# A float64 weight split without a sign pass, weight columns by halves, a third staging place, p in packs, and a new table of ranks

## The chip, the cores and the metric

The kernel runs on one core of one Trainium2 chip. The metric is the device time in microseconds (us), the median of several runs. Matrix products run on PE (TensorE), elementwise work on DVE (VectorE) and ACT (ScalarE), and loads and stores are issued by SP. POOL does almost nothing here. "clock" is the clock that TensorE was granted; its two levels are 2.4 GHz (shown as 1.00) and 1.2 GHz (0.50).

## The reference

`p` holds 32 packed queries for each of 8 x 8 heads. They attend to `k` and `v`, the result serves as keys and values for `q`, and a gated feed-forward layer with a convolution over the sequence follows. The scale factors of the weights are float64 scalars of NumPy, so `w_in`, `conv_w` and `w_out` arrive as float64; `q`, `k`, `v` and `p` are float32.

```python
def sm_attn(qq, kk, vv):
    s = scale * np.matmul(qq, kk.transpose(0, 1, 3, 2))
    s = s - np.max(s, axis=-1, keepdims=True)
    a = np.exp(s)
    a = a / (np.sum(a, axis=-1, keepdims=True) + 1e-09)
    return np.matmul(a, vv)
p_packed = sm_attn(p, k, v)          # q, k, v: 8, 8, 576, 64; p: 8, 8, 32, 64
out = sm_attn(q, p_packed, p_packed)
x = out.transpose(0, 2, 1, 3).reshape(8, 576, 512)
h = np.maximum(x @ w_in, 0.0)        # w_in: 512 x 1024
conv_out = conv_w[0] * h_before + conv_w[1] * h + conv_w[2] * h_after
gate = 1.0 / (1.0 + np.exp(-conv_out))
return (h * gate @ w_out).astype(np.float32)   # w_out: 1024 x 512
```

## The kernel before

**Groups and batches.** The 64 heads are worked on in 16 groups g of four heads; two groups make one of the 8 batches b. For a group, `load_kq` and `load_v` load `k`, `q` and `v`, and `head_transpose` turns `k` and `q` (the first four groups on PE with copies by ACT, the others on DVE). `queries` scales and transposes the packed queries. `attention` does the rest: first scores (tiles `kT`, `pT`), their maximum (`nm` on DVE), the exponential, the product with `v`, second scores (`qT`, `ppT`), and a softmax on DVE and ACT whose last tiles are `a2hi` and `a2lo`, a value and its remainder.

**The feed-forward part.** `packed_weight(b, hf)` multiplies the packed values of a batch with one half of the columns of `w_in` and leaves `ghi` and `glo`. `ffn1(b, j)`, j from 0 to 7, multiplies these with `a2hi` and `a2lo`, applies the ReLU into one of three buffers `hbuf`, and gates it with the convolution's sigmoid into `hgt`. `ffn2(m)`, m from 0 to 35, splits 128 rows of `hgt` into `xhi` (ACT) and `xlo` (DVE) and multiplies them with `wo_hi` and `wo_lo` in 24 matmuls (L720). Its output goes out by DMA.

**The weights.** `load_weight(i)` and `weight(i)` handle eight pieces of 1 MB: four of `w_in`, then four of `w_out`. `f64_parts` splits a float64 piece into float32 parts: ACT scales the high words (L281), and DVE shifts left by 3 (L283), puts the sign bit back (L285), masks the exponent (L289) and scales the low words (L291). PE adds the parts up (L346). The pieces are staged in halves of `hgt[1]` (`spare`), one of them in `w_in_sb`. `packed_weight` waits for all four pieces of `w_in`.

**What sets the order.** `Flow` is a planner in the kernel. Each function yields its work as steps for an engine; whenever an engine is free, the ready step with the lowest number in the table `RANKS` goes next, and the order is then fixed: each engine runs its list in turn, SP its list of loads and stores too. `take` and `give` are buffers handed on: three tiles `kq` for `k` and `q`, two for `v`, three `hbuf` (`h`), and so on. Until the first `ffn2` has been placed, the planner fills gaps of PE with small matmuls on the tile `idle` (L258), which compute nothing that is used.

Of the kernel before, what the change touches and what calls it, by code (L numbers as in the profile page):

```python
# [8 lines left out]
F32 = mybir.dt.float32  # L9
# [12 lines left out]
    k=[-645.37, -581.7, -645.95, -844.11, -379.62, -375.1, -363.45, -47.77, 708.11, 1034.07, -210.35, 1035.0, 2258.89, 1246.95, 2776.42, 5491.81],  # L22
    v=[-634.88, -576.04, -524.23, -352.44, -474.91, 569.37, 815.34, 1122.01, 1500.35, 1611.47, 1083.29, 1634.37, 1803.36, 2006.67, 5057.89, 5016.42],
    q=[-504.47, 5384.4, -435.54, -367.64, -409.72, -123.0, -229.45, 1157.76, 1826.35, 1958.61, 1961.31, 2349.96, 2739.02, 5189.37, 5900.17, 5687.45],
    queries=[-124.07, 4947.56, -576.16, 695.08, -936.2, 3146.3, -805.71, -833.64, 1723.01, 937.55, -839.58, -1636.16, -699.27, 4760.45, 746.56, -516.14],
    kT=[1289.34, 1260.73, 824.17, 1514.37, 3387.98, 1162.59, 1714.67, -880.73, 2085.08, 5733.43, 661.28, -243.54, -133.19, -1560.99, 2719.23, 1444.35],
    qT=[2349.41, -862.23, 1500.3, -520.73, -836.19, 1311.15, 5046.28, 2258.92, 84.63, 1578.67, 2671.05, 1256.34, 4798.98, -604.41, 2193.41, 4803.19],
    attention=[-312.33, 1080.14, -1264.6, -854.22, -833.2, 888.88, 1206.99, 641.08, -62.4, -943.58, 2495.68, -762.92, -896.54, 638.89, -844.03, -837.43],
    sums=[1170.39, 4739.32, 1087.43, -129.08, -833.34, -795.65, -617.55, 732.0, 92.96, 1253.68, 921.66, 4676.98, 2791.9, -198.77, 1508.38, -128.03],
# [1 line left out]
    load=[-1419.97, -236.8, -646.87, 5205.55, 2444.58, -393.65, -586.49, -453.41],
    weight=[958.54, 4407.77, 746.18, 4155.56, 1719.93, 2554.0, -847.43, 4425.27],
    packed=[-838.33, 1929.06, 1148.03, -461.0, 4425.27, 4993.29, 668.7, 1234.53, -222.7, 5473.37, -518.74, 1316.77, 884.48, 5592.56, 5384.7, 1490.18],
    ffn1=[1814.15, -1369.6, -784.93, 4729.05, 5596.18, 845.36, 1618.07, 1158.66, -659.35, 1633.27, 4246.81, -514.28, 1503.84, -125.71, 542.72, -819.28, -857.94, -834.32, 831.55, -551.42, -551.12, -846.96, 1932.67, -543.96, 4461.75, 3236.12, 773.89, -616.98, -320.81, 5019.89, -713.12, -601.27, -1230.08, -655.85, 1159.65, 2700.73, 2122.97, 4279.32, -792.92, 18.96, 1213.31, -1515.25, 5098.64, -153.63, -504.19, -419.06, 1111.01, 1722.91, -533.48, 1251.79, 710.95, -783.68, -384.13, 5910.7, -565.69, 4602.14, 659.94, 497.38, 1568.93, -811.33, 2444.88, 589.46, 5595.83, 4931.48],
# [751 lines left out]
```

## Time and profile before

| | us |
|---|---|
| median of three runs | 434.65 |
| lowest and highest | 433.1 and 435.48 |
| the profiled execution, its own time | 435.47 |
| its span, first to last instruction | 433.6 |

In the profile a busy time is the union of an engine's instructions. Instructions of one engine overlap a little at their edges, so a row's duration is longer than the step from one start to the next. A matmul's end is modelled, so a full PE is not PE at its peak. A wait in brackets names the time that the engine sat idle before an instruction and who ended it. Line numbers are those of the kernel before unless they are said to be of the kernel after.

### The profile page before, as it was taken

The page shows a single profiled execution, that of the slowest core. Times are in us where ns is not written, and L with a number is a line of the kernel's source. Part 1 is how long each engine was busy: PE and PEld are TensorE (multiplying, and loading weights), DVE is VectorE, ACT ScalarE, POOL GpSimd, SP SyncE. Part 2 cuts the span into 40 slices and gives each one's busy share as a digit, 9 for nine tenths or more (in the row PEclk, how much of TensorE's full clock was granted, in tenths as well). Part 3 has the DMA queues.
Part 4 walks back from the last instruction along what each step waited for, and adds up shares of the span by engine and source line. Part 5 has one row for each costly group of instructions (what it writes and reads, how often), then busy time and mean ns, then how long its engine had stood idle before and what let it go on. Part 6 is the DMA issues. An engine that isn't in the chain of part 4 may idle for free.

```text
span 433.6 us, 8375 instructions
## 1 busy us (share of the span) xinstructions
PE 420.9 (97%) x3437; PEld 336.9 (78%) x3437; DVE 351.5 (81%) x497; ACT 321.4 (74%) x509; POOL 1.6 (0%) x13
## 2 busy tenths in 40 slices
PE   5999999799999999999999999999999999999996
PEld 5676878578876987787877888788869787897774
DVE  3479998879999999999999987998688994685220
ACT  4477999886999889878968677888667875673221
POOL 1000000000000000000000000000000000000000
PEclk9999999989999999999999999999999999999999
DMA  8999824499676847791919640700100001000111
GB/s 318 374 318 278 171 81 54 118 160 172 111 135 119 154 70 146 137 164 43 167 60 163 132 80 26 134 27 24 49 26 26 26 24 48 26 24 26 48 50 48
DMA packets 135077, 47.22 MB, mean 109 GB/s; under 512 B 119668, under 2 KB 127860, under 8 KB 134528
## 3 DMA queue, kind: packets, MB, share of 16 engines
q1 hardware_dynamic: 135008, 46.67, 49.3%
q8 instruction: 27, 0.44, 0.5%
q14 instruction: 10, 0.08, 0.1%
q0 software_dynamic: 32, 0.02, 0.0%
HBM read 37.25 MB, written 9.44 MB: 108 GB/s over the span
## 4 chain that ended last, share of the span: by engine, by line
PE 80%; DMA 7%; DVE 6%; ACT 4%; issue 1%; SPq 1%; DVEq 0%; ACTq 0%
PE fo L720 41%; PE big L658 20%; DMA hgt<-in_moe_w_in_dram 4%; PE sm L720 4%; PE big L468 3%; PE big L606 3%; PE sm L533 2%; PE big L346 2%; PE big L524 1%; PE idle L258 1%; DMA q<-in_q_dram 1%; DMA k<-in_k_dram 1%; DVE hgt L675 1%; DVE hgt L685 1%; DVE hgt L679 1%
## 5 line engine op out<-in xcount | busy, mean ns | idle before, releaser
L720 PE MATMUL fo<-wo_hi,xhi 128*128 128x512 f32 x264 | 106.7, 404 | 0.7 <-ACT o L725 0.7
L720 PE MATMUL fo<-wo_hi,xlo 128*128 128x512 f32 x264 | 104.7, 397 | 0.0
L720 PE MATMUL fo<-wo_lo,xhi 128*128 128x512 f32 x264 | 104.0, 394 | 0.0
L704 DVE TENSOR_TENSOR xlo<-hgt,xhi 128x1024 fp32r<-128x1024 f32 (+1 forms) x40 | 44.0, 1106 | 28.6 <-ACT xhi L701 22.1
L720 PEld LDWEIGHTS fo<-wo_hi,xhi 128*128 128x128 f32 x264 | 50.0, 190 | 12.9 <-ACT o L725 2.0
L675 DVE SCALAR_TENSOR_TENSOR hgt<-hbuf,cw,hgt 128x576 f32<-128x576 f32 x64 | 51.6, 813 | 9.5 <-ACT hgt L673 9.3
L720 PEld LDWEIGHTS fo<-wo_hi,xlo 128*128 128x128 f32 x264 | 49.7, 188 | 12.4 <-DVE xlo L704 0.2
L720 PEld LDWEIGHTS fo<-wo_lo,xhi 128*128 128x128 f32 x264 | 49.6, 188 | 9.9
L683 ACT ACTIVATE hgt<-hgt 128x576 f32<-128x576 f32 x64 | 43.4, 684 | 18.4 <-DVE hgt L679 17.9
L658 PE MATMUL big<-a2hi,ghi 128*128 128x288 f32 x256 | 56.1, 300 | 0.3 <-ACT wo_lo L353 0.3
L658 PE MATMUL big<-a2hi,glo 128*128 128x288 f32 x256 | 54.7, 294 | 0.0
L658 PE MATMUL big<-a2lo,ghi 128*128 128x288 f32 x256 | 54.4, 293 | 0.0
L685 DVE TENSOR_TENSOR hgt<-hgt,hbuf 128x576 f32<-128x576 f32 x64 | 47.0, 745 | 9.0 <-ACT hgt L683 8.9
L679 DVE SCALAR_TENSOR_TENSOR hgt<-hbuf,cw,hgt 128x576 f32<-128x576 f32 x64 | 51.0, 809 | 0.6
L669 ACT ACTIVATE hbuf<-big 128x576 f32<-128x576 f32 x64 | 41.4, 653 | 13.0 <-PE big L658 10.2
L673 ACT ACTIVATE hgt<-hbuf,cw 128x576 f32<-128x576 f32 x64 | 49.4, 781 | 0.9
L658 PEld LDWEIGHTS big<-a2hi,ghi 128*128 128x128 f32 x256 | 42.0, 188 | 5.2 <-DVE s L557 0.8
L701 ACT CAST xhi<-hgt 128x1024 fp32r<-128x1024 f32 (+1 forms) x40 | 38.3, 964 | 8.6 <-PE fo L720 4.2
L658 PEld LDWEIGHTS big<-a2lo,ghi 128*128 128x128 f32 x256 | 41.0, 188 | 0.0
L658 PEld LDWEIGHTS big<-a2hi,glo 128*128 128x128 f32 x256 | 40.9, 188 | 0.0
L725 ACT COPY o<-fo 128x512 f32<-128x512 f32 x33 | 19.3, 584 | 24.7 <-PE fo L720 20.3
L258 PE MATMUL idle<-ident 128*128 128x128 f32 x148 | 22.7, 302 | 2.5 <-POOL ident masks.py:199 2.5
(102 smaller groups left out, 595.8 us busy)
## 6 DMA issues: line engine op xcount, KB each, us to landing
out_dram<-o SPq DMA_DIRECT2D x36, 256.0 KB, 2.0
v<-in_v_dram SPq DMA_DIRECT2D x16, 512.0 KB, 4.9
q<-in_q_dram SPq DMA_DIRECT2D x48, 144.0 KB, 4.1
k<-in_k_dram SPq DMA_DIRECT2D x48, 144.0 KB, 4.6
hgt<-in_moe_w_out_dram SPq DMA_DIRECT2D x4, 1024.0 KB, 5.3
...
```

What stands on the lines that cost most here:

```text
L258: nc.tensor.matmul(out=t[:, :128], lhsT=ident, rhs=ident, start=True, stop=True)
L658: nc.tensor.matmul(out=t[:, hf, :SH], lhsT=w[:, gg, js], rhs=x[:, hf * SH : (hf + 1) * SH], start=n == 0, stop=n == 3 * NG - 1,)
L669: nc.scalar.activation(out=h[:, 1 : S + 1].rearrange("c (f s) -> c f s", f=2), in_=t[:, :, :SH], func=AF.Relu)
L673: nc.scalar.activation(out=d, in_=h[:, 1 : S + 1], func=AF.Copy, scale=cw[:, NJ + j : NJ + j + 1])
L675: nc.vector.scalar_tensor_tensor(out=d, in0=h[:, 0:S], scalar=cw[:, j : j + 1], in1=d, op0=ALU.mult, op1=ALU.add)
L679: nc.vector.scalar_tensor_tensor(out=d, in0=h[:, 2 : S + 2], scalar=cw[:, 2 * NJ + j : 2 * NJ + j + 1], in1=d, op0=ALU.mult, op1=ALU.add)
L683: nc.scalar.activation(out=d, in_=d, func=AF.Sigmoid)
L685: nc.vector.tensor_tensor(out=d, in0=d, in1=h[:, 1 : S + 1], op=ALU.mult)
L701: nc.scalar.copy(out=hi[:, :, o], in_=src)
L704: nc.vector.tensor_tensor(out=lo[:, :, o], in0=src, in1=hi[:, :, o].bitcast(F32), op=ALU.subtract)
L720: nc.tensor.matmul(out=t, lhsT=x[:, c, :], rhs=w[:, c, :], start=c + i == 0, stop=c == NJ - 1 and i == 2)
L725: nc.scalar.copy(out=o, in_=t)
```

## The change

Six things are changed. The sign pass on DVE (L285) goes; ACT's scaling becomes a parametric ReLU with `alpha` of -2^32, which for a negative word sets the bit that the shift by 3 then moves into the sign's place. A piece of `w_in` is now a half of the rows by a half of the columns, so that `packed_weight(b, 0)` waits for two pieces and not for four. The pieces are staged in three places (two in `hgt[1]`, one in a tile `stage` of its own), and piece i waits for piece i-3. `p` is loaded in four packs of four groups, in tiles of a ring of two. Some steps must now follow the same step of the group before (`s1`, `hi`, `pk`). And all numbers of `RANKS` are new, so nearly every instruction has another place.

```diff
-    first=[-889.74, 1324.12, -1218.14, -1509.47],
-    hold=375.11,
+    first=[3485.5317, 5992.9594],
+    p=[-602.8021, 423.7176, 2583.1976, 2679.7272],
+    hold=-10.7483,
...
-    p_sb = cpool.tile([128, NGT, D], F32, name="p_sb")
+    stage = cpool.tile([128, 2 * DFF], F32, name="stage")
...
-        | dict(gw=2, h=3, x=2, o=2, tmp_in=2, tmp_out=2),
+        | dict(gw=2, h=3, x=2, o=2),
...
-        nc.scalar.mul(out=e, in_=up.bitcast(F32), mul=F64_REBIAS)
+        nc.scalar.activation(out=e, in_=up.bitcast(F32), func=AF.Prelu, scale=F64_REBIAS, alpha=-(2.0**32))
-        yield Step("DVE", 69 + m * 100 // 96)
-        nc.vector.scalar_tensor_tensor(
-            out=ti, in0=up, scalar=-0x80000000, in1=ti, op0=ALU.bitwise_and, op1=ALU.bitwise_or
-        )
...
-        first = i < NCC
-        c = i if first else 2 * (i - NCC)
-        src = w_in[c * 128 : (c + 1) * 128, :] if first else w_out[c * 128 : (c + 2) * 128, :]
-        raw = src.dtype != F32
-        st = w_in_sb[:, 2:, :].rearrange("r c f -> r (c f)") if i == 2 else spare[:, (0, 1, 0, 0, 1, 0, 1, 0)[i] * 2 * DFF :]
-        return first, c, src, raw, st[:, : 2 * DFF if raw else DFF]
+        c = 2 * (i % 2) if i < 4 else 2 * (i - 4)
+        w, cols = (w_in, slice(i // 2 * 512, i // 2 * 512 + 512)) if i < 4 else (w_out, slice(0, DM))
+        src = w[c * 128 : (c + 2) * 128, cols]
+        n = 2 * DFF if src.dtype != F32 else DFF
+        st = stage if i % 3 == 2 else spare[:, i % 3 * 2 * DFF :]
+        return c, cols, src, st[:, :n]
 
     def load_weight(i):
-        first, c, src, raw, st = weight_tile(i)
-        yield Step("SP", 2600, after=[("wp", (0, 1, 3, 4, 5)[i - 3])] if i >= 3 else [], sets=[("wd", i)])
-        o, a = (st.bitcast(I32), src.bitcast(I32)) if raw else (st, src)
-        if first:
-            nc.sync.dma_start(out=o, in_=a)
+        _, _, src, st = weight_tile(i)
+        yield Step("SP", 2600, after=[("wp", i - 3)] if i >= 3 else [], sets=[("wd", i)])
+        if src.dtype != F32:
+            src, st = src.bitcast(I32), st.bitcast(I32)
+        nc.sync.dma_start(out=st.rearrange("r (c f) -> r c f", c=2), in_=src.rearrange("(c r) f -> r c f", r=128))
+    def weight(i):
+        c, cols, src, st = weight_tile(i)
+        hi, lo = (w[:, 2 * (i % 4) : 2 * (i % 4) + 2, :].rearrange("r c f -> r (c f)") for w in (wo_hi, wo_lo))
+        token, tags = ("gw", ("ghi", "glo")) if i < 2 else ("x", ("xhi", "xlo"))
+        parts = []
+        def tiles():
+            t, e = (wk.tile([128, DFF], F32, name="tmp", tag=tag) for tag in tags)
+            parts.extend([(ident, t), (minus, lo)])
+            return t, e, lo
+        after = [("wd", i), "minus"] + ([("ws", i - 4)] if i >= 4 else [])
+        if src.dtype != F32:
+            yield from f64_parts(tiles, st, DFF, after, [token], [("wp", i)])
         else:
-            nc.sync.dma_start(out=o.rearrange("r (c f) -> r c f", c=2), in_=a.rearrange("(c r) f -> r c f", r=128))
-    def weight(i):
-        first, c, src, raw, st = weight_tile(i)
-        hi, lo = (w[:, c : c + 2, :].rearrange("r c f -> r (c f)") for w in (wo_hi, wo_lo))
-        after = [("wd", i), "minus"] + ([] if first else [("ws", n) for n in range(NCC)])
-        tmp = "tmp_in" if first else "tmp_out"
-        parts = []
-        def tiles():
-            t, e = (wk.tile([128, DFF], F32, name="tmp", tag=tag) for tag in (("ghi", "glo") if first else ("xhi", "xlo")))
-            rest = wk.tile([128, DFF], F32R, name="rest", tag=("xhi", "xlo")[i % 2]) if first else lo
-            parts.extend([(ident, t), (minus, rest)])
-            return t, e, rest
-        if raw:
-            yield from f64_parts(tiles, st, DFF, after, [tmp], [("wp", i)])
-        else:
-            yield Step("DVE", 0, after=after, take=[tmp], sets=[("wp", i)])
+            yield Step("DVE", 0, after=after, take=[token])
             parts.append((ident, st))
-        if not first:
+        if i >= 4:
             yield Step("ACT", 905)
             nc.scalar.copy(out=hi, in_=parts[0][1])
             parts.append((minus, hi))
         ns = 2 * (864 + 234 * (len(parts) - 1))
-        yield Step("PE", ns, take=["big"], give=[tmp], sets=[("ws", i)], cols=2 * (1536 + 512 * len(parts)))
+        yield Step("PE", ns, take=["big"], give=[token], sets=[("ws", i)], cols=2 * (1536 + 512 * len(parts)))
         s = big()
         for hf in range(2):
             for k, (w, x) in enumerate(parts):
                 nc.tensor.matmul(
                     out=s[:, hf, :], lhsT=w, rhs=x[:, 512 * hf : 512 * hf + 512], start=k == 0, stop=k == len(parts) - 1
                 )
-        yield Step("ACT", 905, after=[("wp", 2)] if i == 3 else (), give=["big"], sets=[("w", i)])
-        if first:
-            nc.scalar.copy(out=w_in_sb[:, c, :].rearrange("r (h f) -> r h f", h=2), in_=s)
-        else:
-            nc.scalar.copy(out=lo.rearrange("r (h f) -> r h f", h=2), in_=s)
+        yield Step("ACT", 905, give=["big"], sets=[("w", i)])
+        nc.scalar.copy(out=w_in_sb[:, c : c + 2, cols] if i < 4 else lo.rearrange("r (c f) -> r c f", c=2), in_=s)
...
-    def load_p(i, gs):
-        yield Step("SP", 182 * (gs.stop - gs.start), sets=[("p", g) for g in range(gs.start, gs.stop)])
+    packs = {}
+    def load_p(i):
+        gs = slice(4 * i, 4 * i + 4)
+        yield Step("SP", 730, after=[("pT", g) for g in range(4 * i - 8, 4 * i - 4)] if i >= 2 else (), sets=[("p", i)])
+        packs[i] = wk.tile([128, 4, D], F32, name="p", tag="p")
         nc.sync.dma_start(
-            out=p_sb[:, gs, :], in_=p.rearrange("b h n d -> (b h n) d").rearrange("(g r) d -> r g d", r=128)[:, gs, :]
-        )
-    def gate(g):
-        if g < NG:
-            return []
-        j = (4, 6)[g % NG] if g < 2 * NG else (-1, -1)[g % NG]
-        return [("pT", g - 1)] + ([("f1", g // NG - 1, j)] if j >= 0 else [])
+            out=packs[i], in_=p.rearrange("b h n d -> (b h n) d").rearrange("(g r) d -> r g d", r=128)[:, gs, :]
+        )
 
     def queries(g):
-        yield Step("ACT", 200, after=[("p", g)] + gate(g), take=["pm"])
+        yield Step("ACT", 200, after=[("p", g // 4)] + [("pT", g - 1)] * (g > 0), take=["pm"])
         pm = wk.tile([128, 2, D], F32, name="pm", tag="pm")
-        nc.scalar.mul(out=pm, in_=p_sb[:, g, :].unsqueeze(1).broadcast_to([128, 2, D]), mul=SCALE)
+        nc.scalar.mul(out=pm, in_=packs[g // 4][:, g % 4, :].unsqueeze(1).broadcast_to([128, 2, D]), mul=SCALE)
...
-        yield Step("PE", 556, after=[("pT", g), ("kT", g)], take=["big", "a1"], give=["kT", "pT"], cols=1152, tiled=True)
+        yield Step("PE", 556, after=[("pT", g), ("kT", g)] + [("s1", g - 1)] * (g > 0), take=["big", "a1"], give=["kT", "pT"], sets=[("s1", g)], cols=1152, tiled=True)
...
-        yield Step("ACT", 573, take=["a2"])
+        yield Step("ACT", 573, after=[("hi", g - 1)] * (g > 0), take=["a2"], sets=[("hi", g)])
...
-        after = [("pp", g) for g in gs] + [("w", c) for c in range(NCC)]
-        yield Step("PE", 905, after=after, take=["big", "gw"], give=["ppT"] * NG if hf else (), cols=2048, tiled=True)
+        i = 2 * b + hf
+        after = [("pk", i - 1)] * (i > 0) + [("pp", g) for g in gs] + [("w", 2 * hf), ("w", 2 * hf + 1)]
+        yield Step("PE", 905, after=after, take=["big", "gw"], give=["ppT"] * NG if hf else (), sets=[("pk", i)], cols=2048, tiled=True)
```

What that does to the order is shown at three places. The first is SP's list of loads at the start of the program. Before:

```order
L314 DMA hgt_77<-in_moe_w_in_dram 128x2048
L481 DMA p_sb<-in_p_dram 128x2x64
L418 DMA k<-in_k_dram 128x1152
L314 DMA w_in_sb<-in_moe_w_in_dram 128x2048
L418 DMA k<-in_k_dram 128x1152
L418 DMA hgt_76<-in_k_dram 128x1152
L402 DMA v<-in_v_dram 128x4x256
L406 DMA v<-in_v_dram 64x4x64
```

After, where `hgt_77` is `hgt[1]`:

```order
L477 DMA p<-in_p_dram 128x4x64
L410 DMA q<-in_q_dram 128x1152
L410 DMA hgt_76<-in_k_dram 128x1152
L410 DMA k<-in_k_dram 128x1152 x2
L410 DMA hgt_76<-in_k_dram 128x1152
L410 DMA hgt_76<-in_q_dram 128x1152
L477 DMA p<-in_p_dram 128x4x64
L312 DMA hgt_77<-in_moe_w_in_dram 128x2x1024
L394 DMA v<-in_v_dram 128x4x256
```

Before, a piece of `w_in` led and a second one stood fourth; now a pack of `p` leads, six loads of `k` and `q` follow, and the first piece of `w_in` stands behind them and a second pack.

The second place is DVE's list between the maximum `nm` of the second group and the first softmax on second scores (`s`, from L557, after L547). Before, with the third piece of `w_in` (`rest` is its low part):

```order
L513 TENSOR_REDUCE nm<-big 128x1
L283 TENSOR_SCALAR tmp<-tmp 128x1024
L285 SCALAR_TENSOR_TENSOR tmp<-hgt_77,tmp 128x1024
L593 TENSOR_SCALAR rs<-sm_307 128x1
L289 TENSOR_SCALAR tmp<-tmp 128x1024
L595 RECIPROCAL rs<-rs 128x1
L291 SCALAR_TENSOR_TENSOR rest<-hgt_77,tmp 128x1024
L557 STREAM_TRANSPOSE s_377<-big 128x576
```

After, with the first piece, whose low part is kept in `wo_lo` for a while:

```order
L503 TENSOR_REDUCE nm<-big 128x1
L285 TENSOR_SCALAR tmp<-tmp 128x1024
L287 TENSOR_SCALAR tmp<-tmp 128x1024
L583 TENSOR_SCALAR rs<-sm_274 128x1
L289 SCALAR_TENSOR_TENSOR wo_lo<-hgt_77,tmp 128x1024
L585 RECIPROCAL rs<-rs 128x1
L547 STREAM_TRANSPOSE s_345<-big 128x576
```

The sign pass of L285 is gone, and the piece that stands here is the first one and not the third.

The third place is PE's list from the second scores of an early group to the first `packed_weight` (`w_in_sb`, `ppT`) and behind it. Before:

```order
L452 MATMUL big<-ident,q 128x128 x4
L258 MATMUL idle<-ident 128x128 x4
L606 MATMUL big<-w_in_sb,ppT 32x512 x16
L258 MATMUL idle<-ident 128x128 x3
L622 MATMUL big<-ghi,minus 128x512 x2
```

After:

```order
L460 MATMUL big<-qT,ppT 32x288 x8
L259 MATMUL idle<-ident 128x128 x2
L444 MATMUL big<-ident,q 128x128 x5
L597 MATMUL big<-w_in_sb,ppT 32x512 x8
L523 MATMUL sm<-v,a1T 32x64 x20
L444 MATMUL big<-ident,q 128x128 x4
L514 MATMUL big<-ident,a_467 128x128 x5
L613 MATMUL big<-ghi,minus 128x512 x2
L539 MATMUL sm<-ident,pb 128x128
L341 MATMUL big<-tmp,ident 128x512
```

Before, fillers on `idle` stood between these steps and the first `ffn1` came behind them with three rows between; now work of later groups (`v`, `q`, `a`, `pb`) stands there, and the first `ffn1` comes 24 rows later.

## Rows read from the trace of the kernel before

**Rows 1.** The page: engines over the span, and the clock in 40 slices:

```profile
PE 420.9 (97%) x3437; PEld 336.9 (78%) x3437; DVE 351.5 (81%) x497; ACT 321.4 (74%) x509; POOL 1.6 (0%) x13
...
PEclk9999999989999999999999999999999999999999
```

**Rows 2.** Chain of waits, in order of time: start, us, engine, tile, line:

```profile
80.52 5.29 DMA q<-in_q_dram
...
92.66 0.70 PE fo L720 x3
...
365.57 1.58 PE big L658 x12
...
424.26 5.66 PE sm L720 x24
...
429.99 0.59 ACT o L725
```

**Rows 3.** Busy time by stretch: PE, PEld, DVE, ACT, POOL, clock, DMA share, GB/s:

```profile
0.00:92.42 92.42, 84.19 (x821) 62.97 (x821) 70.82 (x103) 72.16 (x117) 1.59 (x13) 0.98 0.75 212
92.42:140.67 48.25, 48.12 (x485) 37.24 (x486) 46.52 (x73) 42.37 (x77) 0.00 (x0) 1.00 0.79 135
140.67:430.00 289.33, 288.57 (x2134) 236.69 (x2133) 234.12 (x323) 206.31 (x317) 0.00 (x0) 1.00 0.38 72
```

**Rows 4.** DVE's busy time by stretch: length, busy, clock, DMA share, GB/s:

```profile
0.00:85.27 85.27, 65.73 (x97) 1.00 0.73 217
85.27:140.67 55.40, 51.62 (x81) 0.97 0.80 138
```

**Rows 5.** Groups by line on DVE and ACT, busy us, mean ns, idle before:

```profile
L285 DVE SCALAR_TENSOR_TENSOR tmp<-hgt,tmp 128x1024 int32<-128x1024 int32 x7 | 8.5, 1215 | 0.1
L281 ACT ACTIVATE tmp<-hgt 128x1024 f32<-128x1024 f32 x7 | 8.2, 1166 | 4.2 <-DMA hgt<-in_moe_w_in_dram 4.2
L673 ACT ACTIVATE hgt<-hbuf,cw 128x576 f32<-128x576 f32 x64 | 49.4, 781 | 0.9
L683 ACT ACTIVATE hgt<-hgt 128x576 f32<-128x576 f32 x64 | 43.4, 684 | 18.4 <-DVE hgt L679 17.9
```

**Rows 6.** Timeline of DVE: start, us, instruction, idle before:

```profile
6.88 0.69 DVE L283 TENSOR_SCALAR tmp<-tmp 128x1024 int32<-128x1024 int32 x1 [6.88 <-ACT tmp L281]
...
61.50 0.69 DVE L283 TENSOR_SCALAR tmp<-tmp 128x1024 int32<-128x1024 int32 x1
62.10 0.81 DVE L675 SCALAR_TENSOR_TENSOR hgt<-hbuf,cw,hgt 128x576 f32<-128x576 f32 x1
62.83 1.22 DVE L285 SCALAR_TENSOR_TENSOR tmp<-hgt,tmp 128x1024 int32<-128x1024 int32 x1
63.97 0.81 DVE L679 SCALAR_TENSOR_TENSOR hgt<-hbuf,cw,hgt 128x576 f32<-128x576 f32 x1
...
85.27 1.21 DVE L704 TENSOR_TENSOR xlo<-hgt,xhi 128x1024 fp32r<-128x1024 f32 x1
```

**Rows 7.** All engines by stretch, columns as in Rows 3: the early loads:

```profile
0.00:20.00 20.00, 15.21 (x83) 11.26 (x84) 9.01 (x14) 8.46 (x16) 1.59 (x13) 1.00 0.93 339
20.00:46.10 26.10, 25.61 (x294) 18.42 (x292) 21.56 (x35) 20.53 (x34) 0.00 (x0) 1.00 1.07 291
92.00:110.00 18.00, 18.00 (x130) 14.49 (x123) 17.14 (x30) 13.78 (x28) 0.00 (x0) 1.00 0.98 155
```

**Rows 8.** Timeline, one load of k behind the transpose that frees its tile:

```profile
112.64 1.37 DVE L441 STREAM_TRANSPOSE qT<-q 128x1152 f32<-128x1152 f32 x1
...
121.82 1.38 DVE L441 STREAM_TRANSPOSE kT<-k 128x1152 f32<-128x1152 f32 x1 [0.86 <-DMA k<-in_k_dram]
```

**Rows 9.** All engines by stretch, columns as in Rows 3: the clock:

```profile
0.00:2.00 2.00, 0.00 (x0) 0.00 (x0) 0.00 (x0) 1.26 (x1) 1.21 (x12) 1.00 0.20 33
84.00:86.00 2.00, 0.37 (x9) 0.24 (x10) 2.00 (x4) 0.99 (x3) 0.00 (x0) 1.00 0.39 92
88.00:90.00 2.00, 2.00 (x54) 1.41 (x60) 0.01 (x1) 1.85 (x5) 0.00 (x0) 0.50 1.39 192
```

More of the change, by code (lines that the diff above doesn't have):

```diff
@@ L21 @@
 RANKS = dict(
[L22 to L29, printed above, removed]
@@ L30 @@
-    first=[-889.74, 1324.12, -1218.14, -1509.47],
[L31 to L34, printed above, removed]
@@ L35 @@
-    ffn2=[5203.6, 4556.28, 5345.44, 5173.21, -722.08, 4872.4, 553.25, -91.92, -841.77, -610.15, 4839.75, 918.51, -364.57, -807.95, 894.01, 3501.6, 5449.81, 1443.86, -1242.77, -881.89, 1233.64, -1220.43, 939.27, -491.71, 926.3, 4842.53, -594.64, -1460.55, 4327.4, -642.08, -596.16, 1098.16, 1166.02, 4809.51, -390.18, 1487.96],
-    hold=375.11,
+    k=[-411.0614, -56.32, -268.848, -369.0188, -10.607, 1.2892, 3.3386, 133.9183, 102.8098, 879.0292, 1255.3289, -152.1904, 3265.748, 2301.2373, 4073.7935, 5527.8193],
@@ new lines @@
+    kT=[5736.7974, -483.8463, 553.7556, 408.255, 3083.2521, 5765.4763, 3896.7744, 5207.2595, 5358.4206, 3202.632, 5269.8891, 5371.5274, 5299.2063, 120.4482, 1271.3159, 2568.6227],
+    qT=[1822.3814, 149.2968, 1218.3584, -269.2693, 1711.232, 1654.8561, 2171.3878, 3701.8394, 5672.096, 353.4709, 4066.7032, 5429.4678, 2268.9292, 5358.7206, 222.3705, 2101.3936],
+    attention=[551.6318, 5443.0779, 4911.4625, 3277.6066, 65.8326, -4.185, 2216.4119, 775.0971, 3.0273, -63.566, 3554.4746, 194.6953, -141.7721, 2717.9598, 5675.3416, 2685.8275],
@@ new lines @@
+    sums=[2212.5273, 6593.67, 2120.4894, 2288.466, 2267.3881, 3298.9219, 539.0862, 5551.4175, 278.5043, 4140.9774, 2298.0652, 5441.9071, 5447.2342, 5340.7613, 2224.1344, 2195.0737],
+    first=[3485.5317, 5992.9594],
+    p=[-602.8021, 423.7176, 2583.1976, 2679.7272],
+    load=[539.5951, 5201.6034, 3915.0356, -142.7698, -520.5537, 6101.7696, 3.6438, 3085.3699],
+    weight=[3894.055, 415.5091, 5692.3927, 1094.9361, 2353.1416, 3840.1368, 5430.0718, 5676.1554],
+    packed=[3577.1581, 5645.4193, 6697.6272, 2233.1226, 823.9014, 5464.0982, 4050.5266, 1240.3014, 1363.631, -311.5196, 5146.9566, 223.8075, 1458.215, 3320.7258, -22.7754, 5405.3068],
@@ new lines @@
+    ffn1=[382.8943, -307.4377, 670.6109, 3512.0211, 3061.8509, -696.3821, 708.7212, -523.2062, 2230.3122, 778.609, 3794.9833, 1385.1523, 171.9222, 5875.7606, 5891.3708, -268.9693, -27.916, 229.1412, 6086.4179, 3961.4117, 1253.6236, -298.9416, -92.0749, 506.8444, 1021.7865, 2235.1843, 1822.6814, 1818.6582, 289.8734, -373.3513, 123.6805, 971.6445, -505.8058, 2261.7916, 2059.7915, 2244.506, 2287.2636, 3251.6386, 4026.9332, 3882.595, 5829.3173, 1396.2015, 3883.7763, 6025.1134, -420.7776, 1005.7303, 426.1176, 4453.7934, 4265.8601, 1304.3038, 25.1843, -325.5138, 2534.8185, 47.5927, 5893.1673, 5388.9951, 5605.6557, 107.7366, 46.4049, 2226.8256, 5622.8384, 5211.2071, -79.5994, 387.443],
@@ L37 @@
+    ffn2=[3213.9683, 5587.2785, -45.6475, 2059.3311, 5970.2991, -826.7935, 1356.9098, 2161.583, -208.5721, 5444.3776, 960.4174, 2239.558, 966.066, 1050.7084, 5488.7732, 3774.109, 1199.7934, 5443.758, 5765.0603, 2151.9103, 5849.4642, 5597.3931, 4837.0348, -88.4009, 3979.5915, 2137.3678, 245.2455, 3761.219, 176.6706, 5898.133, 5524.2367, 204.1131, 1753.915, 261.0496, 165.4131, 5407.7056],
+    hold=-10.7483,
 )
@@ L277, in f64_parts @@
         low = pair[:, :, 0].bitcast(U32)
-        yield Step("ACT", 93 + m * 5 // 6, after=after, take=take)
+        yield Step("ACT", 93 + m * 14 // 15, after=after, take=take)
         t, e, rest = tiles()
         ti, ei = t.bitcast(I32), e.bitcast(I32)
-        nc.scalar.mul(out=e, in_=up.bitcast(F32), mul=F64_REBIAS)
+        nc.scalar.activation(out=e, in_=up.bitcast(F32), func=AF.Prelu, scale=F64_REBIAS, alpha=-(2.0**32))
         yield Step("DVE", 68 + m * 100 // 192)
         nc.vector.tensor_scalar(out=ti, in0=ei, scalar1=3, scalar2=None, op0=ALU.logical_shift_left)
-        yield Step("DVE", 69 + m * 100 // 96)
-        nc.vector.scalar_tensor_tensor(
-            out=ti, in0=up, scalar=-0x80000000, in1=ti, op0=ALU.bitwise_and, op1=ALU.bitwise_or
-        )
         yield Step("DVE", 68 + m * 100 // 192)
@@ L689, in ffn2 @@
         bs = range(m * 128 // S, ((m + 1) * 128 - 1) // S + 1)
-        after = [("hg", b, j) for b in bs for j in range(NJ)] + [("w", i) for i in range(NCC, 2 * NCC)]
+        after = [("hg", b, j) for b in bs for j in range(NJ)] + [("w", i) for i in range(4, 8)]
         if m:
@@ L740, in tile_packed_attention_conv_gate @@
         add("sums", g, sums(g))
-    add("first", 0, load_p(0, slice(0, NG)))
-    add("first", 1, load_p(1, slice(NG, NGT)))
-    add("first", 2, conv_weight())
-    add("first", 3, identities())
-    for i in range(2 * NCC):
+    add("first", 0, conv_weight())
+    add("first", 1, identities())
+    for i in range(NGT // 4):
+        add("p", i, load_p(i))
+    for i in range(8):
         add("load", i, load_weight(i))
```

3 lines of the change are left out of this document (added).

## The prediction

> **What bounds the kernel now.** I read the page first: PE is busy for 97% of the span, DVE for 81%, ACT for 74%, and the clock is 0.9 or more in nearly all slices [rows 1]. A busy PE can hold fillers, so I read the chain of waits next. It goes back over a load of `q` (80.52 us) to the first weights, and from the first `ffn2` matmuls, at about 92.4, it is PE almost without a break up to 429.99, where the last copy and store begin [rows 2]. The stretches say the same: from 92.42 to 140.67 PE is busy 48.12 of 48.25 us, from there to 430 288.57 of 289.33, at a clock of 1.00 [rows 3]. So the time is three pieces: 92.4 us until `ffn2` starts, 337.6 us of full PE, 3.6 us of copy and store (to the span's 433.6). Only the first piece has slack. What PE does is the same in both kernels apart from fillers, so a gain can come from one place: useful PE work must lie ahead of 92.4, or that point must come earlier.
>
> What sets that point is DVE more than PE. Ahead of its first `xlo` (85.27) DVE is busy for 65.73 us, and from there to 140.67 for 51.62 of 55.40 [rows 4]; so also behind 92.4 DVE has only 3.8 us to spare until the fifth row tile of `ffn2`, which starts at 140.67. A change that only let PE start earlier would be held there by DVE.
>
> **The change part by part.** *The sign pass.* Eight instructions of 1.215 us go [rows 5]; in a full queue one costs its step, 1.14 us (62.83 to 63.97, [rows 6]), so 9.1 us of DVE, all ahead of the first `xlo`. A ninth, on the convolution weights, is small. What ACT pays: the scaling stays one instruction. No row shows a parametric ReLU. The scaling takes 1.166 us; at 576 elements a sigmoid takes 0.684 and a copy with a scale per partition 0.781 [rows 5], so a function need cost nothing and another operand about 0.1. The bound is 0 to 0.1 us for each of eight, and no gain, since nothing is taken from the instruction. I take 0, by the sigmoid. A table load would cost more, but the order has 30 loads before and after, and none at the scaling.
>
> The scaling row shows ACT doing at once what DVE would do in a further pass of 1.14 us. The Trainium skill, ScalarE: Activation LUTs, section "Rules for kernel authors", says the opposite way round that ReLU and multiplications belong on VectorE. By that rule the pass would stay where it was and the sum below would lose its 9.1 us; by the rows the pass is free on ACT, since the instruction is there anyhow and ACT is not the fuller engine.
>
> *More work ahead of the first `xlo`.* The order after has 109 DVE rows ahead of it, and not 97. Nine of L285 are gone, and 21 are new: the softmax of two more groups (17 rows), two rows on first scores, two of convolution. At a row's step (duration less 0.08, as 0.81 for 0.73 in [rows 6]) the 97 rows make 63.2 us and the 109 make 65.3. So DVE is 2.1 us longer there, not 9 shorter. But PE gets work for it: ahead of the first `ffn2` the order after has three more `ffn1` (1.58 each, [rows 2]), one score, and some transposes and remainders, 6.7 us together. Behind that point there are then 337.6 - 6.7 = 330.9 us of PE work left.
>
> *When DVE gets there.* Before, 85.27 - 63.2 = 22.1 us passed without a DVE step, 6.9 of them ahead of the first weight [rows 6]. After, `p` and six loads of `k` and `q` are ahead of the first piece of `w_in`: 4.85 MB must have landed, and not 1.05. At the 339 GB/s of the first 20 us [rows 7] that is 14.3 us; before, the first piece was used at 5.7 (its scaling of 1.17 ends ahead of 6.88 [rows 6]), 2.6 later than this rate says, so 14.3 to 16.9. I take 15.5, then 0.9 until ACT is through with the rows ahead, and 1.1 for the scaling: DVE's first long weight step at 17.5, with 2.3 us of other steps behind it. That is 15.2 us lost at once, more than before. From there I laid the lists of the four engines side by side, each row at its step: DVE waits 1.2 us for the second scores of the first group, 0.8 for the scaling of the third piece, 1.1 for the first `a2hi`, 0.8 for the scaling of the first piece of `w_out`, and then is full. Several of these loads land within a microsecond of their use, and PE's short steps in the first 20 us may run at the lower clock, so I add 2.4. Without a step: 15.2 + 3.9 + 2.4 = 21.5. First `xlo` at 65.3 + 21.5 = 86.8, `ffn2` at 88.0 with the 1.1 of `xlo` and a hand-over.
>
> *The rest.* The two `w_in` halves, the third place and the packs cost nothing by themselves: same bytes, same PE rows, same copies; what they change is the order. Their cover is the queue of loads: if SP is held, as by the wait of the third pack for four `pT` copies, every load behind it is late. By the lists these copies are done some 5 us before SP comes there. Between the first and the fifth tile of `ffn2`, the order has 39.1 us of DVE steps beside 40.1 of PE, so DVE may lose 1 us there without harm; before it lost 3.8 [rows 4]. I take 2.0, so PE waits 1.0.
>
> **Sum.** 88.0 + 330.9 + 1.0 = 419.9 for PE's end; + 3.6 = 423.5 for the span; the profiled execution took 435.47 for a span of 433.6, so + 1.9 = 425.4, 10.1 less. The median of the runs shown is 434.65, so **424.5**. Both bounds: without the 2.4 and the 1.0, and with no time lost by a load, 421; with ACT's eight at 0.1 each, the first piece at 16.9 and another 2 us of waits, 428.7.
>
> **The rivals.** *Loads bind (0.16).* With its strided loads of `k` the chip moved 155 GB/s at a DMA share of 0.98 [rows 7]. The `k` of the fifth group stands behind 15.5 MB in SP's list. At 291 GB/s from 25.5 us on (8.7 MB moved) it lands at 49, just when DVE, in order, wants it; at 229 GB/s, about midway to 155, at 55. DVE then stands 6 us, and `ffn1` with it: 430.5. For it: the early loads are in one list. Against: DMA was not idle-free before either (0.93 and 1.07 as share).
>
> *The ring of `kq` binds (0.06).* A `k` loaded early, by SP's list, is used only in the eighth group, and holds one of three tiles until then. Before, 7.8 us passed from the end of a transpose (114.0) to the landing of the load that it let go (121.82, [rows 8]). Four loads after have 4 to 7 us of DVE steps for that, so DVE stands 3 to 7 us in all. DVE's margin over PE is 2 to 4 us there, so 427 to 430.
>
> *It is slower: the clock (0.06).* After 2 us in which PE was busy 0.37, the clock was 0.50 two slices later [rows 9]. The order has 74 fillers before and 29 after. At the lower level each PE step doubles. Ahead of the first `ffn1` there are 35.3 us of PE work in some 52 us, so 16.3 of the doubling fit into gaps; all of it at 0.50 gives 19 us more, 443. It decides the sign from 12 us on, that is from some 28 of these 35 us at the lower level. Against: work of later groups stands in the fillers' place, and the first 2 us show 1.00 with an idle PE [rows 9]. The Trainium skill, TensorE: Matmul & The Clock Gate, section "HAM oscillation — how this bites in real kernels", says that gaps between short stretches of matmuls throttle the clock again and again; by it this case is the likely one, by the page's clock row, 0.9 up to 80 us [rows 1], it is not.
>
> *It does not do what it says (0.04).* The ReLU costs a table switch or a slower pass after all, or the new order loses what DVE gains: 433 to 437.
>
> **How the numbers follow.** Forecast (421 to 428.7): 0.66; below it, if the lists run without any late load: 0.02. A measurement of this kernel can tell about 0.5% (2.2 us) from no change. Faster by more than that, below 432.4: 0.66 + 0.02 + 0.15 of the loads' case + 0.05 of the ring's, 0.88. Within 0.5%: 0.05, from the last case and the ends of others. Slower: 0.07, the clock and a part of the last. The range reaches over the loads' case and the ring's: 419.5 to 431.
>
> **What would show it.** First scores at about 10 us; the first weight step of DVE at 17.5; the first `ffn1` at 51 to 54; the first `xlo` at 86 to 88, `ffn2` at 88 and PE full from there; DVE's busy time lower by 9.8; the scaling at 1.17 us. It is wrong if DVE stands for loads between 40 and 60 us, if the clock lies at 0.5 beyond 20 us, or if PE waits for `xlo` behind the fifth tile.

## The result, and the profile after

The kernel after takes 429.11 us (median), the kernel before in the same comparison 434.88: a ratio of 0.9871, 95% interval 0.9838 to 0.9905, so 5.6 us off the 434.65 that the prediction starts from. The forecast was 10.1. The direction held. The time lies 0.4 us above the upper end of the sum's own bounds, 428.7, and inside the stated range only because that reaches over the cases of the loads and of the ring as well. Nearly half of the gain is missing, and the experiments show that one premise of the sum was wrong.

The profiled execution took 428.88 us for a span of 426.9. First the page of the kernel after, its engines and the clock, beside [rows 1]:

```profile
PE 410.5 (96%) x3347; PEld 325.6 (76%) x3347; DVE 342.4 (80%) x488; ACT 322.1 (75%) x509; POOL 1.6 (0%) x13
...
PEclk9999999999999999999999999999999999999999
```

DVE lost 9.1 us, ACT gained 0.7, PE lost 10.4. PE's fillers alone shrank by 12.2, from 22.7 to 10.5 us. The next rows are the filler groups, of before and of after (count, ns min/median/max, first and last start):

```profile
L258 PE MATMUL idle<-ident x148: 270/275/581, 2.5 to 80.6; 128*128 128x128 f32 x148
```

```profile
L259 PE MATMUL idle<-ident x58: 271/275/582, 3.7 to 82.0; 128*128 128x128 f32 x58
```

Then the chain of waits of the kernel after (start, us, what), which answers to [rows 2]:

```profile
31.78 6.34 DMA q<-in_q_dram
...
42.62 3.26 SPq L421
45.93 3.45 SPq L421
49.43 4.90 DMA k<-in_k_dram
...
54.53 1.39 DVE kT L433
...
57.26 3.21 PE big L649 x24
...
70.87 0.86 PE idle L259 x6
...
80.86 1.10 PE big L597 x16
81.96 0.64 ACT hbuf L660
...
102.25 1.58 PE big L649 x12
...
417.73 5.62 PE sm L711 x24
...
423.42 0.58 ACT o L716
```

Between the landing of that `k` and 104 us DVE stands in the chain with one transpose only. From 56.06 to 81.96 the chain runs over PE, fillers included, from there over ACT to 101.87, and then over PE again.

And the kernel after cut where its `ffn2` starts (PE, PEld, DVE, ACT, POOL, clock, DMA share, GB/s), beside [rows 3]:

```profile
0.00:91.88 91.88, 80.32 (x790) 56.56 (x790) 68.84 (x109) 75.11 (x129) 1.58 (x13) 1.00 0.84 225
91.88:139.90 48.02, 47.42 (x453) 38.06 (x452) 45.75 (x68) 40.59 (x72) 0.00 (x0) 1.00 0.79 135
139.90:423.34 283.44, 282.76 (x2109) 230.98 (x2107) 227.78 (x313) 205.80 (x309) 0.00 (x0) 1.00 0.35 70
```

This says where the time went. `ffn2` starts at 91.88 instead of 92.42 [rows 3], which is 0.54 us earlier. From there PE runs to 417.73 + 5.62 = 423.35, that is 331.47 us; before it ran from 92.42 to 424.26 + 5.66 = 429.92 [rows 2], 337.50 us. So 6.03 of the 6.59 us between the two profiled executions are PE work that now lies ahead of `ffn2`, in the place of fillers. The start itself, for which the prediction had 4.4 us, gave half a microsecond.

Why it did not come earlier is seen in DVE's timeline (start, us, instruction, idle before), and in SP's queue:

```profile
18.83 0.69 DVE L285 TENSOR_SCALAR tmp<-tmp 128x1024 int32<-128x1024 int32 x1
...
54.53 1.38 DVE L433 STREAM_TRANSPOSE kT<-k 128x1152 f32<-128x1152 f32 x1 [2.50 <-DMA k<-in_k_dram]
...
90.76 1.23 DVE L695 TENSOR_TENSOR xlo<-hgt,xhi 128x1024 fp32r<-128x1024 f32 x1
```

```profile
22.59 8.13 SPq L421 DMA_DIRECT2D k<-in_k_dram  x4
30.83 0.86 SPq L312 DMA_DIRECT2D hgt<-in_moe_w_in_dram  x1
31.78 0.41 SPq L410 DMA_DIRECT2D q<-in_q_dram  x1
...
42.02 8.27 SPq L421 DMA_DIRECT2D k<-in_k_dram  x4
```

The first long weight step came at 18.83 and the first `xlo` at 90.76. In between DVE stood 2.50 us for the `k` of the fifth group, whose four transfers took SP 8.27 us to issue. DVE standing for a load between 40 and 60 us is one of the prediction's own signs of being wrong. The first `ffn1`, expected at 51 to 54, starts at 57. The strided `k` ahead of the fourth piece of `w_in` (22.59) is one that nobody needs for long: it belongs to the twelfth group, the eighth of those loaded with strides; the prediction calls it the eighth group's. From 60 us on, three engines are full at once (columns as above):

```profile
60.00:70.00 10.00, 9.97 (x102) 7.95 (x108) 9.82 (x19) 9.94 (x17) 0.00 (x0) 1.00 1.04 123
70.00:80.00 10.00, 10.00 (x73) 7.75 (x58) 10.00 (x15) 10.00 (x16) 0.00 (x0) 1.00 0.29 70
80.00:90.00 10.00, 9.35 (x74) 6.08 (x73) 10.00 (x14) 9.94 (x15) 0.00 (x0) 1.00 0.18 30
```

### The profile page after: what moved, and what is told of

Read it like the earlier page. It is cut to its first block, busy times and chain, and to the rows that moved or that the text cites. A ratio compares the mean times of both kernels' runs of the same rounds, so it can differ in the third digit from the quotient of the medians.

```text
span 426.9 us, 8189 instructions
## 1 busy us (share of the span) xinstructions
PE 410.5 (96%) x3347; PEld 325.6 (76%) x3347; DVE 342.4 (80%) x488; ACT 322.1 (75%) x509; POOL 1.6 (0%) x13
## 4 chain that ended last, share of the span: by engine, by line
PE 83%; ACT 8%; DMA 5%; SPq 2%; DVE 1%; issue 1%; DVEq 0%; ACTq 0%
PE fo L711 42%; PE big L649 22%; PE sm L711 4%; PE big L460 3%; PE big L597 3%; PE sm L523 2%; PE big L514 2%; SPq L421 2%; DMA q<-in_q_dram 1%; DMA hgt<-in_k_dram 1%; PE big L341 1%; PE big L444 1%; DMA k<-in_k_dram 1%; PE idle L259 1%; DMA out_dram<-o 1%
## 5 line engine op out<-in xcount | busy, mean ns | idle before, releaser
L674 ACT ACTIVATE hgt<-hgt 128x576 f32<-128x576 f32 x64 | 43.5, 685 | 10.6 <-DVE hgt L670 10.1
L692 ACT CAST xhi<-hgt 128x1024 fp32r<-128x1024 f32 (+1 forms) x40 | 38.2, 963 | 17.5 <-PE fo L711 15.8
## 6 DMA issues: line engine op xcount, KB each, us to landing
hgt<-in_moe_w_out_dram SPq DMA_DIRECT2D x3, 1024.0 KB, 10.4
```

The source lines that it names most:

```text
L674: nc.scalar.activation(out=d, in_=d, func=AF.Sigmoid)
L692: nc.scalar.copy(out=hi[:, :, o], in_=src)
```

## The experiments

Theory A was the prediction's: DVE sets the point at which `ffn2` starts. Its first rival, B, was that the loads do. In each experiment the order of the other instructions is the one of its base kernel: the planner still counts the steps that are left out. All ratios are to the kernel before on the same chip, where it took 433.59 us (experiments 1 to 4), 433.80 (5 to 8) and 434.08 (9 to 12), so ratios are compared and not times. The start of `ffn2` is read from one profiled execution each.

**1. The pass put back into the kernel after**

```diff
-nc.scalar.activation(out=e, in_=up.bitcast(F32), func=AF.Prelu, scale=F64_REBIAS, alpha=-(2.0**32))
+nc.scalar.mul(out=e, in_=up.bitcast(F32), mul=F64_REBIAS)
...
+nc.vector.scalar_tensor_tensor(out=ti, in0=up, scalar=-0x80000000, in1=ti, op0=ALU.bitwise_and, op1=ALU.bitwise_or)
```

> The kernel after, in its own order, with the sign set again by a DVE instruction behind the shift (1.215 us each, a step of 1.14, eight times) and a plain scaling on ACT. Theory A, DVE sets the point at which ffn2 starts: 9.1 us of DVE come back ahead of the first xlo; the wait for the k of the fifth group (2.50 us) and up to 1.5 us of others are filled by it, so 5 to 9 us more: 434 to 438. Theory B, the loads set that point and DVE has room: the pass falls into DVE's waits, 429 to 430.5. Either way the first ACT step on the weights stays at about 1.16 us; if the parametric ReLU cost ACT something, a part would come back here.

Measured: 432.45 us, ratio 0.9973 (0.9962 to 0.9985). Against the 0.9871 of the kernel after, the pass costs 1.0% in the new order, 4.4 us (0.6 to 1.5% between the ends of the two intervals). The first `xlo` is at 95.61 and `ffn2` at 96.64, 4.8 later. That is less than the 9.1 us of the instructions: by B's side of it, the 2.50 us for `k` are filled, and theory A's range was 5 to 9. The time lies between the ranges of A and B. In this run DVE is full from 60 us on (columns as above), here, with the pass, it is the fullest engine, and the chain of waits runs over it from 51.99 to 91.00:

```profile
60.00:70.00 10.00, 9.74 (x93) 7.73 (x92) 9.97 (x20) 9.01 (x16) 0.00 (x0) 1.00 0.90 170
70.00:80.00 10.00, 10.00 (x70) 7.62 (x71) 10.00 (x16) 10.00 (x17) 0.00 (x0) 1.00 0.60 96
80.00:90.00 10.00, 8.80 (x69) 7.06 (x67) 9.97 (x14) 9.41 (x14) 0.00 (x0) 1.00 0.01 2
```

The run also shows what the new order alone is worth, with the pass in it: 0.27%, 1.2 us.

**2. The sign in ACT's scaling, in the kernel before, and nothing else**

```diff
-nc.scalar.mul(out=e, in_=up.bitcast(F32), mul=F64_REBIAS)
+nc.scalar.activation(out=e, in_=up.bitcast(F32), func=AF.Prelu, scale=F64_REBIAS, alpha=-(2.0**32))
...
-nc.vector.scalar_tensor_tensor(out=ti, in0=up, scalar=-0x80000000, in1=ti, op0=ALU.bitwise_and, op1=ALU.bitwise_or)
```

> The kernel before, in its own order, with only the sign moved to ACT's scaling: the pass of eight times 1.14 us is gone from DVE and nothing else is moved. Theory A, DVE sets the start of ffn2 (85.27 us for the first xlo): 9.1 us less, 425 to 427. Theory B, the new order is needed to get the gain, since the loads of the old order (a q that landed at 80.5, in the chain of waits) hold DVE anyway: 430 to 433.

Measured: 434.10 us, ratio 1.0014 (0.9999 to 1.0030). No gain, and also not the 430 to 433 of theory B. This is where theory A falls for the kernel before: 9.1 us of DVE are gone and `ffn2` starts at 92.47 instead of 92.66 in the chain (start, us, what; line numbers are shifted by three):

```profile
80.08 5.53 DMA q<-in_q_dram
...
92.47 0.70 PE fo L717 x3
```

**3. One load moved in the kernel after.** When the planner has placed the `k` of the twelfth group, its transfers are issued only behind those of the fifth group's `k`:

```diff
+            if step.sets == [("k", 11)]:
+                late = s[1]
+                self.streams.remove(s)
+                continue
             following = next(s[1], None)
...
+            if step.sets == [("k", 4)]:
+                next(late, None)
```

> The kernel after with one load moved in SP's list: the strided k of the twelfth group, which stands ahead of the fourth w_in load, comes behind the k of the fifth group. All compute engines keep their order. Theory A, DVE's wait of 2.50 us at 54.5 and the 0.8 to 1.1 us of PE and ACT for q and the fourth piece are owed to that load in SP's list: the k of the fifth group is issued some 8 us earlier, the wait goes, 425 to 427. Theory B, it is owed to the rate at which all bytes come, or DVE stands for something else at once: 428 to 429.5.

Measured: 427.40 us, ratio 0.9861 (0.9844 to 0.9877), next to 0.9871: the difference is inside the intervals, and the time lies between the ranges of A and B. In the profiled execution `ffn2` starts at 90.43, 1.45 us earlier. The trace shows why so little came of it. The `k` is there in time, and its transpose stands at 51.46 without a wait (54.53 in the kernel after); DVE's next wait is for the next piece of weight, one of `w_out`, whose load stands behind both `k` in SP's queue (DVE's timeline, then SP's queue of this run):

```profile
51.46 1.37 DVE L439 STREAM_TRANSPOSE kT<-k 128x1152 f32<-128x1152 f32 x1
...
57.79 0.69 DVE L291 TENSOR_SCALAR tmp<-tmp 128x1024 int32<-128x1024 int32 x1 [1.58 <-ACT tmp L289]
```

```profile
41.95 7.87 SPq L427 DMA_DIRECT2D k<-in_k_dram  x8
49.93 2.18 SPq L318 DMA_DIRECT2D hgt<-in_moe_w_out_dram  x1
```

So the wait for `k` was owed to the place in SP's list, as expected, but it was not worth its length.

**4. A further DVE pass left out of the kernel after**

```diff
-nc.vector.tensor_scalar(out=ei, in0=ti, scalar1=-0x800000, scalar2=None, op0=ALU.bitwise_and)
+if m < 1024:
+    nc.vector.tensor_scalar(out=ei, in0=ti, scalar1=-0x800000, scalar2=None, op0=ALU.bitwise_and)
```

> The kernel after without the second shift-and-mask pass of DVE on each of the eight weight pieces (0.68 us each, steps of 0.61; the mask is left out and the rest of the pass is computed from the unmasked word, so the high parts keep their numbers and the low parts are multiplied by other words). Theory A, DVE still sets the start of ffn2 after the change: 4.9 us off DVE and 3.5 to 5 us off the time, 424 to 425.6. Theory B, after the change the loads or ACT set it: under 1 us, 428 to 429.3.

Measured: 429.29 us, ratio 0.9902 (0.9882 to 0.9921). No gain, as theory B had it. The same engine from which 9.1 us were worth 4.4 has 4.9 more to give away for nothing. The trace shows a reason: in the kernel after six of the eight masks lie ahead of the `k` of the fifth group (the last two start at 60.92 and 80.05), and with them gone DVE stands for that `k` again:

```profile
55.12 1.38 DVE L434 STREAM_TRANSPOSE kT<-k 128x1152 f32<-128x1152 f32 x1 [2.78 <-DMA k<-in_k_dram]
```

What is taken off DVE ahead of the load falls into its waits, and only the two masks behind it, 1.2 us, could have moved the start. So DVE's work ahead of that load does not set the start any more; what its work behind the load is worth this run does not show.

With A fallen for the kernel before, the other engines ahead of `ffn2` come in. In the kernel before from 40 to 80 us (columns as above) ACT is busy for 39.60 of 40 us, PE with its fillers for 38.61, DVE for 37.19:

```profile
40.00:80.00 40.00, 38.61 (x314) 30.19 (x298) 37.19 (x51) 39.60 (x59) 0.00 (x0) 1.00 0.50 114
```

Theory C: ACT and DVE hold each other; taken alone, neither gives anything. D: ACT alone. E: a `q` in SP's list. F, added for the last four: the fillers, which stand as a fixed number in PE's list, hold the old pace too; K: without them the clock falls.

**5 to 8. ACT relieved, with and without relief for DVE.** In the first batch the centre tap of the convolution is left out on ACT:

```diff
-nc.scalar.activation(out=d, in_=h[:, 1 : S + 1], func=AF.Copy, scale=cw[:, NJ + j : NJ + j + 1])
+if b > 0:
+    nc.scalar.activation(out=d, in_=h[:, 1 : S + 1], func=AF.Copy, scale=cw[:, NJ + j : NJ + j + 1])
...
-in1=d, op0=ALU.mult, op1=ALU.add
+in1=d if b else h[:, 1 : S + 1], op0=ALU.mult, op1=ALU.add
```

> The kernel before, in its own order, with ACT relieved and DVE not: the centre tap of the convolution on the eight tiles of the first batch (a copy with a scale, 0.78 us, a step of 0.70, all eight ahead of the first xlo) is left out and its weight taken as 1, so ACT has 5.6 us less. Theory C, ACT and DVE are both full ahead of ffn2 (ACT 9.8 to 9.95 of 10 us in each stretch from 40 to 80, DVE 9.6 to 9.97 from 30 to 70), so that one alone gives little: 432 to 433.6. Theory D, ACT alone sets the start of ffn2: 428 to 430. Theory E, SP's list does (the q that is issued at 80.5 behind a v): 433 to 434.

Before, ACT alone: 433.49 us, 0.9982 (0.9966 to 0.9998).

> The kernel before with both: the sign in ACT's scaling and so no pass on DVE (9.1 us less), and the eight centre taps of the first batch left out (5.6 us less on ACT, their weight taken as 1). Theory C, both engines bind together: 4 to 5.6 us off, 428 to 430, where each alone gave next to nothing. Theory D, ACT alone: the same as with the centre taps alone. Theory E, the q behind a v in SP's list holds PE anyway: 432 to 434.

Before, ACT and DVE: 432.96 us, 0.9977 (0.9963 to 0.9992). Theory C expected 428 to 430 here, so C is not enough either; D falls with the run ahead of it. Theory E's range holds, and the chains show what its `q` waits for: in SP's list it stands behind a `v`, and the `v` is issued when PE has run the `sm` matmuls that free its tile. What leads up to those is ACT in experiment 2, from 66.66 to 77.29, and in experiment 5, with ACT relieved, PE with its fillers, from 47.91 on (chain of waits of experiment 5):

```profile
67.10 1.34 PE idle L258 x12
...
77.52 0.88 PE sm L533 x40
...
78.41 0.38 SPq L402
...
80.16 5.23 DMA q<-in_q_dram
```

> The kernel after, in its own order, with ACT relieved alone: the eight centre taps of the first batch left out, their weight taken as 1, 5.6 us off ACT ahead of the first xlo. Theory C: DVE is at 10.00 of 10 us from 70 to 90 and takes over, up to 1.5 us, 427.5 to 429. Theory D, ACT alone binds after the change: 424 to 426. Theory B, the loads: 428.3 to 429.3.

After, ACT alone: 428.30 us, 0.9871 (0.9846 to 0.9897), the ratio of the kernel after itself. D falls here too; the ranges of B and C both hold.

> The kernel after with both engines relieved: the mask pass left out on the eight weight pieces (4.9 us off DVE; the low parts are multiplied by unmasked words) and the eight centre taps of the first batch left out, their weight taken as 1 (5.6 us off ACT). Theory C: 3.5 to 5 us off, 424 to 425.6, where the mask alone gave nothing. Theory B, the loads of w_out and of the fifth group set the start of ffn2 whatever ACT and DVE cost: 427.5 to 429.

After, ACT and DVE: 427.30 us, 0.9853 (0.9836 to 0.9870), again hardly told from it. Theory C's 424 to 425.6 is missed; B's 427.5 to 429 is nearly met. With both relieved the chain goes back from `ffn2` over PE alone, to the `k` of the fifth group (chain of waits of this last run):

```profile
50.51 4.88 DMA k<-in_k_dram
...
58.31 3.20 PE big L650 x24
...
91.75 0.70 PE fo L713 x3
```

From 57.11 to 91.75 PE is never idle, and some 3 us of that are fillers (20 matmuls). So in the kernel after the start of `ffn2` has three covers: PE's list with ACT's behind it, as in its own chain, and DVE's, over which the chain runs in experiments 1 and 7. The load of that `k` lies ahead of PE's and DVE's.

**9 to 12. Fewer fillers**

```diff
             self.tiled = False
-            self.warm(n)
+            if until < 20000:
+                self.warm(n)
```

> The kernel before, in its own order, without the fillers that its plan puts behind 20 us (45 of 74 stay out, some 14 to 15 us of PE). It is the comparison for the next two. Theory F, the fixed list of fillers keeps PE at 9.6 to 10 of 10 us from 30 to 80 and with it the old pace: here little happens, since ACT and DVE are as full, 432 to 433.8. Theory K, without them the clock falls to 0.50 for a stretch: over 436.

Before, fillers alone: 433.84 us, 0.9994 (0.9978 to 1.0010). The trace has 38 filler matmuls for 148, two to a filler, so 55 of 74 stayed out (the expectation says 45) and some 15 us of PE. Theory K holds by half: the clock falls to 0.50 in three stretches where the kernel before has 1.00, but the time stays far from K's 436 (stretches of this run):

```profile
36.00:38.00 2.00, 2.00 (x4) 1.01 (x3) 2.00 (x6) 0.78 (x2) 0.00 (x0) 0.50 0.93 340
70.00:72.00 2.00, 2.00 (x11) 2.00 (x10) 2.00 (x5) 1.99 (x5) 0.00 (x0) 0.50 1.15 168
84.00:86.00 2.00, 2.00 (x57) 1.08 (x41) 2.00 (x3) 1.70 (x4) 0.00 (x0) 0.50 0.32 123
```

The kernel before has one such stretch ahead of `ffn2` [rows 9]. So the ratio holds both what PE won without these fillers and what it lost by the lower clock, and the two are not separated.

> The kernel before with the sign in ACT's scaling and so without the pass, and without the fillers behind 20 us. Theory F, the fillers hid what the pass is worth: 4 to 8 us below the kernel before, 426 to 430. Theories C and E, ACT is full or the q behind a v in SP's list holds PE: 432 to 433.8, as with the fillers. Theory K: over 436.

Before, without the pass too: 433.76 us, 1.0006 (0.9978 to 1.0034). Theory F alone falls: ACT is at 39.70 of 40 us here, and the chain runs over it from 66.05 to 79.97.

> The kernel before with all three covers taken away: no pass on DVE (sign in ACT's scaling, 9.1 us), the eight centre taps of the first batch left out on ACT (their weight taken as 1, 5.6 us), no fillers behind 20 us. Theories F and C together, the three engines held one another: 4 to 7 us below the kernel before, 427 to 430. Theory E, SP's list sets the start of ffn2: 431.5 to 433.

Before, all three: 429.56 us, 0.9885 (0.9850 to 0.9921). Here the gain appears, 1.15% or 5 us; theory E falls with it, since the same `q` in the same place of SP's list now comes earlier; in the chains of experiments 9 to 11 it does not stand any more. `ffn2` starts at 87.07 (chain of waits, and the stretch from 40 to 80 us):

```profile
87.07 0.70 PE fo L719 x3
```

```profile
40.00:80.00 40.00, 35.27 (x273) 25.21 (x263) 34.41 (x50) 37.44 (x57) 0.00 (x0) 0.93 0.56 139
```

> The kernel after with the k of the twelfth group loaded behind that of the fifth and without the fillers behind 20 us (18 to 20 of them, 6 to 7 us of PE). With that k in its old place PE was full from 57 to 92 us with 4 us of fillers in it. Theory F, PE's list is what holds the start of ffn2: 3 to 4 us below the run with the k later (427.4), 423.5 to 424.5. Theory C, ACT and DVE are full there too: 426 to 427.4. Theory K, the clock falls in the gaps: over 429.

After, with the `k` later and few fillers: 426.45 us, 0.9820 (0.9789 to 0.9852). It is the fastest of all, 1.8% below the kernel before; its interval just touches that of the kernel after, so how much of it lies beyond that one stays open. `ffn2` starts at 89.89. PE now has gaps, and DVE and ACT are full (stretches of this run):

```profile
70.00:80.00 10.00, 9.26 (x62) 6.46 (x61) 10.00 (x16) 9.97 (x16) 0.00 (x0) 1.00 0.15 48
80.00:90.00 10.00, 8.79 (x63) 6.52 (x62) 10.00 (x14) 9.94 (x14) 0.00 (x0) 1.00 0.29 45
```

So F's 3 to 4 us were too much: PE's list was one of the covers, and with it thinned the other two are left.

The kernel before and its variants in one table (busy time from 40 to 80 us, of 40; start of `ffn2` by its first row in the chain):

| kernel before, less | PE | DVE | ACT | `ffn2` | ratio |
|---|---|---|---|---|---|
| nothing | 38.61 | 37.19 | 39.60 | 92.66 | 1 |
| pass | 38.74 | 32.94 | 39.60 | 92.47 | 1.0014 |
| ACT's taps | 39.70 | 37.87 | 35.75 | 91.21 | 0.9982 |
| pass, ACT's taps | 39.52 | 33.91 | 35.97 | 91.17 | 0.9977 |
| fillers | 34.52 | 35.75 | 39.33 | 92.17 | 0.9994 |
| fillers, pass | 31.76 | 33.05 | 39.70 | 90.13 | 1.0006 |
| fillers, pass, ACT's taps | 35.27 | 34.41 | 37.44 | 87.07 | 0.9885 |

In each row but the last one engine is left at 39.3 us or more, and the time has hardly moved; in the last no engine is above 37.5, and it has, with a clock of 0.93 in that stretch. The row before the last shows a start 2.5 us earlier in its one profiled execution (432.96 us), but the executions of that kernel run from 432.75 to 437.39, so nothing is read from that. Fillers and taps left out with the pass kept in was not run: that it takes all three, and not those two, is not shown.

## Why the prediction was right in direction and wrong in size

*What bounds the kernel.* "From there on PE is full" was right, to a few tenths: from the start of `ffn2` to the last matmul it takes some 337 us in the old order and 331.5 in the new, in the kernel after as in experiments 1, 3 and 12, wherever the start lies. The next sentence, "What sets that point is DVE more than PE", is **the step that failed**. In its place the runs show three engines nearly full there, ACT for 39.60, PE with its fillers for 38.61 and DVE for 37.19 of 40 us; of the combinations that were run in the old order, only the one with all three relieved lowered the time, by 1.15%. I had read DVE's stretch [rows 4] and not ACT's; [rows 3] already has ACT at 72.16 against DVE's 70.82 us ahead of `ffn2`. ACT's 74% on the page [rows 1] hides a stretch at 99%. Experiment 2 took the sum's first term by itself and measured zero.

*The sign pass.* 9.1 us of steps off DVE: its busy time fell by 9.1 too, from 351.5 to 342.4, where the prediction's sign was 9.8. ACT's price of zero: the scaling with the parametric ReLU takes, from the two staging places (ns min/median/max),

```profile
L283 ACT ACTIVATE tmp<-hgt x6: 1131/1160/1182, 17.6 to 68.7; 128x1024 f32<-128x1024 f32 x6
L283 ACT ACTIVATE tmp<-stage x2: 1173/1173/1173, 23.6 to 43.8; 128x1024 f32<-128x1024 f32 x2
```

against a mean of 1166 [rows 5]. The instructions were priced rightly; what they are worth to the kernel was not: 0 in the old order, 4.4 us in the new. The Trainium skill, ScalarE: Activation LUTs, section "Rules for kernel authors", would leave the ReLU and the multiplication on VectorE; by the 1.160 us row ACT does both at the price of one here, and experiment 1 shows that it pays once the order leaves DVE the fullest engine.

*More work ahead of the first `xlo`.* Right: 109 DVE rows, and `ffn2`'s start to PE's end came out at 331.5 us where 330.9 + 1.0 stood. That term made 5.7 of the forecast 10.1 us, and the measured one 6.03.

*When DVE gets there.* The mis-sized term. Without a step 21.5 us were forecast; by the first `xlo` at 90.76 and the 65.3 us of steps it was 25.5. Of the 4.0 us, 1.3 lie at the first weight step (18.83 for 17.5) and 2.5 at the wait for `k`; the other waits and gaps came to 6.5, near the 3.9 + 2.4. But even this reading flatters the sum: taking that wait away (experiment 3) moved the next one into its place.

*The rivals.* The loads' case, with a chance of 0.16, is the one that came in part: the fifth group's `k` landed at 54.33, where its bounds were 49 and 55, DVE stood for 2.5 us and not 6, and the time lies nearer to its 430.5 than to the forecast of 424.5. The ring of `kq` did not bind: behind 92 us PE waits 1.3 us in all. The clock did not either: `PEclk` is 9 in all 40 slices, with 58 fillers where 148 stood. The Trainium skill, TensorE: Matmul & The Clock Gate, section "HAM oscillation — how this bites in real kernels", made this the likely case; by the rows of experiment 12, with still fewer fillers, the clock is 1.00 in each stretch from 60 to 90 us. In the old order experiment 9 shows such falls, to 0.50 three times, and no lost time. What no rival held was the case that happened: several full engines side by side, where a relief for one is taken up by the next.
